# Sequence 0: the last of its four pairs of heads in float16 parts

## The chip, the cores and the metric

The kernel runs on one core of one Trainium2 chip. What counts is the device time of one execution in microseconds. The kernel before was timed in three runs; their median is 1101.2 us (1100.18 to 1104.09).

## The reference

Eight sequences of 576 tokens go through an attention layer with eight heads of 64 channels, and its output through a feed-forward layer (FFN). Each head mixes causal softmax attention with a retrieval from a memory that came in with the sequence:

```python
scores = scale * np.matmul(q, k.transpose(0, 1, 3, 2))
scores = np.where(causal, -1000000000.0, scores)
a = np.exp(scores - scores.max(-1, keepdims=True))
a /= a.sum(-1, keepdims=True) + 1e-09
local = np.matmul(a, v)
q_p = phi(q)                                   # where(q > 0, q, exp(q) - 1) + 1
mem_out = einsum(q_p, M_prev) / (einsum(q_p, z_prev) + 1e-06)
attn = g * mem_out + (1 - g) * local           # g = sigmoid(beta), one per head

h = x @ w_in                                   # 4608 x 512 by 512 x 2048
out = (h * np.clip(h + 3.0, 0.0, 6.0) / 6.0) @ w_out
```

Input and output are float32, except the two FFN weights, which arrive as float64. The kernel works with float16 pairs: a number is a scaled upper half plus a lower half, and a product takes two or three matmuls.

## The kernel before, in words

**Attention.** The 576 tokens of a sequence make five blocks of 128 (the last has 64). Heads go in pairs of two, since two heads of 64 channels fill 128 partitions; pair p is 0 to 3. A *unit* is one head of one pair for one group of query blocks, and the groups are (0, 1), (2,), (3,) and (4,). The units of a sequence follow each other group by group, in each group pair by pair, in each pair head 0 and head 1: 32 units to a sequence. The names carry these numbers, sequence_group_pair_head: sT_0_2_1_0 holds the scores of sequence 0, group (3,), pair 1, head 0.

A unit goes through these steps: `scores` on TensorE (transposed, keys on partitions), `reduce` (a maximum over key blocks on VectorE, for block 0 a copy on ScalarE, then a maximum over partitions on GpSimd, into mb), `sub` on VectorE, `exp` on ScalarE, `pv` on TensorE (values and memory into o), and for the second head `combine`, which divides and adds both heads' parts into x. For sequences from 1 on the exponentials are also split: `exp` makes the upper half ah on GpSimd, `lo` the lower half al on VectorE.

**Two forms of operands.** For sequence 0 all four pairs use float32 operands straight from the load ("nat"). Each pair lies in one of the first four of six slots of SBUF, is loaded in two parts (256 tokens, then 320), and needs only phi(q) in two parts (`nat_phi`, two passes of ScalarE and one of VectorE to a part). For the later sequences `prep_steps` prepares a pair in ten steps: load q, k and v into staging tiles; magnitude passes on ScalarE and a maximum over partitions on GpSimd; scales; then k, q, phi(q) and v are split into two halves (ScalarE the upper, VectorE the lower), and SP copies the halves of k, q and phi(q) into the slot, four copies for each of them. `mem_steps` does the like for the sequence's memory.

**FFN.** Tokens go in 18 blocks of 256. Block 0 (NNAT = 1) is computed in float32: x is transposed by TensorE in two halves (columns of pairs 0 and 1, and of pairs 2 and 3) and copied to x32 by ScalarE; `ffn1` makes eight steps ph_0_0 to ph_0_14 of eight matmuls each, `ffn2` eight steps of four matmuls for two outputs po_0_0 and po_0_1. The float32 weights come out of the float64 words by `w_decode`: 16 chunks, each with a pass of ScalarE (L643), two of VectorE (L644, L645) and a magnitude pass of ScalarE (L646). A raw chunk waits in W2 or in slots 4 and 5; the buffer is loaded again (L630) after that magnitude pass. Later the weights are split too.

**What sets the order.** A scheduler orders each engine's instructions by priorities that the code sets with `at(...)`, by dependencies, and by its own estimate of times. FFN pieces get priorities by block and step, attention units by their due time. On the chip each engine's queue, SP's for the DMAs too, then runs in that order: an instruction that waits holds what is behind it.

## Time and profile before

| | |
|---|---|
| median of three runs | 1101.2 us |
| profiled execution, its own time | 1104.08 us |
| its span on the core | 1102.4 us |
| TensorE (PE) busy | 1071.2 us, 97% |
| VectorE (DVE) busy | 893.0 us, 81% |
| ScalarE (ACT) busy | 789.0 us, 72% |
| GpSimd (POOL) busy | 405.2 us, 37% |
| bytes read from and written to HBM | 48.14 MB, 9.44 MB |

A busy PE is not a PE at its peak: matmuls are pipelined, and their records overlap. What one costs where PE is full is read from start to start of rows, or from a long row with its count. A float32 matmul leaves two records. PEclk is the granted TensorE clock; where the profile has no record of it, it prints full clock, so the spacing of matmuls tells more there. DMA issues stand on SP's queue (SPq), and a long row there is an issue that waits for its buffer.

### The profile page before, as it was taken

The numbers are of one execution on the slowest core, as the hardware profiler recorded it, in microseconds if no ns is written. First come the engines' busy times: TensorE is split into PE (matmuls) and PEld (weight loads), VectorE is DVE, ScalarE is ACT, GpSimd is POOL, SyncE is SP. The second block draws the span as 40 slices with busy tenths as digits, with TensorE's granted clock in tenths as the row PEclk, the third lists the DMA queues.
The fourth block names the chain that finished last, engine by engine and source line by source line (L and its number), as shares of the span: only waits on it lengthen the run. The fifth ranks groups of instructions, "written<-read, shape, count | busy, mean of one in ns | idle before, by whom it ended". The sixth has DMA issues, their size and how long they took to land.

```text
span 1102.4 us, 28691 instructions
## 1 busy us (share of the span) xinstructions
PE 1071.2 (97%) x10728; PEld 788.6 (72%) x10728; DVE 893.0 (81%) x2350; ACT 789.0 (72%) x1884; POOL 405.2 (37%) x544
## 2 busy tenths in 40 slices
PE   7999999899999999999999999999999999999998
PEld 6888758586767776776768686768686858685664
DVE  5989779899899979998989896999699868792321
ACT  4778769778888878788877887778687857563322
POOL 2322123445455434533344533453244433350000
PEclk9999999999999999999999999999999999999999
DMA  8835452334333432443433432332432230101100
GB/s 251 313 110 174 108 148 78 77 85 102 102 97 97 98 106 78 117 92 101 103 102 47 136 99 51 81 102 76 128 82 68 52 77 14 29 10 31 30 10 20
DMA packets 101467, 101.38 MB, mean 92 GB/s; under 512 B 50256, under 2 KB 80976, under 8 KB 101328
## 3 DMA queue, kind: packets, MB, share of 16 engines
q1 hardware_dynamic: 101328, 99.56, 33.6%
q8 instruction: 84, 1.38, 0.6%
q14 instruction: 55, 0.45, 0.1%
HBM read 48.14 MB, written 9.44 MB: 52 GB/s over the span
## 4 chain that ended last, share of the span: by engine, by line
PE 39%; DVE 18%; ACT 5%; issue 5%; DMA 4%; POOL 1%; SPq 1%; DVEq 0%; ACTq 0%; POOLq 0%
PE po L565 6%; PE po L567 6%; PE po L566 6%; PE ph L542 5%; PE ph L543 5%; PE ph L544 5%; DVE rm L371 3%; DVE a L379 3%; DVE al L398 3%; DVE r L551 2%; DVE g L553 2%; PE sT L354 1%; PE sT L355 1%; PE o L425 1%; PE o L423 1%
## 5 line engine op out<-in xcount | busy, mean ns | idle before, releaser
L373 POOL PARTITION_ALL_REDUCE mb<-rm x256 | 253.9, 992 | 354.5 <-DVE rm L371 249.8
L542 PE MATMUL ph<-x,W 128*128 128x256 f16 x1088 | 296.6, 273 | 3.0 <-DMA x<-W 2.2
L543 PE MATMUL ph<-x,W 128*128 128x256 f16 x1088 | 296.6, 273 | 0.0
L544 PE MATMUL ph<-x,W 128*128 128x256 f16 x1088 | 296.6, 273 | 0.0
L565 PE MATMUL po<-W,g 128*128 128x512 f16 x544 | 206.2, 379 | 5.0 <-ACT ot L573 3.5
L567 PE MATMUL po<-W,g 128*128 128x512 f16 x544 | 206.2, 379 | 0.9 <-DVE g L553 0.9
L566 PE MATMUL po<-W,g 128*128 128x512 f16 x544 | 206.2, 379 | 0.0
L390 POOL TENSOR_SCALAR_AFFINE_SELECT ah<-a 128x384 f16<-128x384 f32 (+2 forms) x224 | 138.3, 619 | 183.0 <-ACT a L386 124.3
L386 ACT ACTIVATE a<-a,scal 128x384 f32<-128x384 f32 (+2 forms) x224 | 141.0, 631 | 63.1 <-DVE a L379 54.1
L379 DVE TENSOR_TENSOR a<-sT,mb 128x128 f32<-128x128 f32 (+3 forms) x320 | 148.3, 479 | 25.6 <-POOL mb L373 19.7
L398 DVE TENSOR_TENSOR al<-a,ah 128x384 f16<-128x384 f32 (+2 forms) x224 | 135.5, 605 | 10.7 <-POOL ah L390 9.9
L371 DVE TENSOR_REDUCE rm<-sT 128x128 f32<-128x256 f32 (+3 forms) x256 | 135.0, 527 | 8.3 <-ACT rm L369 3.8
L551 DVE SCALAR_TENSOR_TENSOR r<-r,ph 128x512 f32<-128x512 f32 x136 | 92.0, 677 | 52.5 <-ACT r L550 51.9
L550 ACT ACTIVATE r<-ph,bias_g,gsc 128x512 f32<-128x512 f32 x136 | 106.4, 783 | 33.2 <-PE ph L544 29.4
L355 PE MATMUL sT<-slot 128*128 128x128 f16 (+1 forms) x840 | 126.7, 210 | 0.0
L354 PE MATMUL sT<-slot 128*128 128x128 f16 (+1 forms) x840 | 124.2, 210 | 1.9 <-DVE a L379 1.4
L542 PEld LDWEIGHTS <-W 128*128 128x128 f16 x1088 | 106.4, 98 | 18.1 <-issue 3.0
L423 PE MATMUL o<-slot,ah 128*128 128x65 f16 (+1 forms) x840 | 116.1, 196 | 3.2 <-POOL ah L390 1.6
L543 PEld LDWEIGHTS <-W 128*128 128x128 f16 x1088 | 106.3, 98 | 15.7 <-issue 1.1
L424 PE MATMUL o<-slot,ah 128*128 128x64 f16 (+1 forms) x840 | 115.2, 195 | 0.0
L455 ACT ACTIVATE x<-o,cf 128x64 f32<-128x64 f32 (+1 forms) x280 | 88.0, 314 | 37.4 <-DVE cf L442 37.2
L544 PEld LDWEIGHTS <-W 128*128 128x128 f16 x1088 | 106.3, 98 | 11.7
(157 smaller groups left out, 2297.3 us busy)
## 6 DMA issues: line engine op xcount, KB each, us to landing
slot<-q SPq DMA_DIRECT2D x112, 144.0 KB, 2.5
out<-ot SPq DMA_DIRECT2D x36, 256.0 KB, 2.0
stv<-vn SPq DMA_DIRECT2D x28, 320.0 KB, 3.5
W<-w_in SPq DMA_DIRECT2D x8, 1024.0 KB, 11.2
slot<-w_out SPq DMA_DIRECT2D x8, 1024.0 KB, 5.0
stq<-qT SPq DMA_DIRECT2D x28, 288.0 KB, 3.1
stk<-kT SPq DMA_DIRECT2D x28, 288.0 KB, 3.2
slot<-k SPq DMA_DIRECT2D x112, 72.0 KB, 2.0
```

Source lines behind the costliest of these rows:

```text
L371: DVE.tensor_reduce(rm[:, m0:m0 + nq], src.rearrange("p (t q) -> p q t", q=nq), axis=AX.X, op=ALU.max)
L373: POOL.partition_all_reduce(mb[:, 0:self.m], rm[:, 0:self.m], P, RMAX)
L379: DVE.tensor_tensor(a[:, c0:c0 + w].rearrange("p (t q) -> p t q", q=nq), self.sT[:, c0:c0 + w].rearrange("p (t q) -> p t q", q=nq), self.m ...
L386: self.exp_ins = ACT.activation(a, a, AF.Exp, scale=slots[self.b, self.p]["esc"], bias=LN_SA)
L390: POOL.affine_select(self.ah[:, 0:self.n], a, pattern=[[0, self.n]], compare_op=ALU.is_ge, fill=0.0, base=1, channel_multiplier=0)
L398: DVE.tensor_tensor(self.al[:, 0:n], self.a[:, 0:n], self.ah[:, 0:n], op=ALU.subtract)
L542: PE.matmul(ph[:, m], wh, f["xh"][:, c], start=c == 0, stop=False)
L543: PE.matmul(ph[:, m], wh, f["xl"][:, c], start=False, stop=False)
L544: PE.matmul(ph[:, m], wl, f["xh"][:, c], start=False, stop=c == 3)
L565: PE.matmul(po, gh[:, m, ts], W2[:, m, 0:512], start=m == 0, stop=False)
L566: PE.matmul(po, gh[:, m, ts], W2[:, m, 512:], start=False, stop=False)
L567: PE.matmul(po, gl[:, m, ts], W2[:, m, 0:512], start=False, stop=m == 15)
```

## The change

Pair 3 of sequence 0 takes the path of the later sequences: loaded whole and split by `prep_steps`, ahead of the order in which the others are. Only pairs 0 to 2 (NATP) stay float32. Sequence 0's memory is needed in both forms, so `mem_steps(0)` runs too, into space that the float32 slots 0 and 2 leave free; its results go under mem["split"]. The loads of pair 3 and of the memory come fourth in LOADS, ahead of pair 2's; two tables of step numbers, PREP_0 and MEM_0, place the other steps at units 0 to 4. Mask operands move from slot 3 to slot 1.

```diff
+NATP = 3
...
-LOADS = ((0, 0), (3, 0), (0, 1), (0, 2), (0, 3), (2, 0), (2, 1), (1, 0), (1, 1), (2, 2), (1, 2), (1, 3), (2, 3))
-B_T = (2, 3, 4, 5)
+LOADS = ((0, 0), (3, 0), (0, 1), (4, 3), (0, 2), (2, 0), (2, 1), (1, 0), (1, 1), (2, 2), (1, 2), (2, 3))
+B_T = (2, 3, 4)
+
+PREP_0 = (0, 0, 1, 1, 2, 2, 2, 3, 4, 4)
+MEM_0 = (0, 0, 1, 2)
...
+        if i == 0:
+            m16_raw = free.bitcast(F32)[:, 0:H * (D + 1)]
+        elif i == 2:
+            m16 = free[:, 0:2 * H * (D + 1)].rearrange("p (x h e) -> p x h e", x=2, h=H)
...
+            self.nat = b == 0 and p < NATP
...
-            if self.b == 0:
+            if self.nat:
                 return
             self.ah = p2.tile([P, 512], F16, name=f"ah_{self.id}", tag="ah")
...
-            mt = mem[b]["t"]
+            mt = mem[b if self.nat else b or "split"]["t"]
...
+        elif x == 4:
+            prep0 = prep_steps(0, n)
+            mem0 = mem_steps(0)
+            prep0[0]()
+            mem0[0]()
...
-    for p in range(NP):
+    for p in range(NATP):
         nat_phi(p, 0)
...
+        for fs0, ks in ((mem0, MEM_0), (prep0, PREP_0)):
+            for f, k in zip(fs0[1:], ks[1:]):
+                if k == t:
+                    at(due(t))
+                    f()
```

What the change makes of the engines' queues is not in these lines, so three places are shown, as the two programs issue them. Line numbers of the changed program are 10 or 11 higher.

The first is ACT, around pair 3's first units. Here W1 from W2 (L643, L654) is a weight chunk's first pass, W2,am1 from W1 (L646, L657) its magnitude pass, rm the copy of block 0's scores, a the exponential, x2 the copy of transposed x. Before:

```order
L643 ACTIVATE W1_95<-W2_96 128x1024
L646 ACTIVATE W2_96,am1_189<-W1_95 128x1024
L643 ACTIVATE W1_95<-W2_96 128x1024
L369 ACTIVATE rm_0_0_3_1_426<-sT_0_0_3_1_413 128x128
L646 ACTIVATE W2_96,am1_189<-W1_95 128x1024
L386 ACTIVATE a_0_0_3_0_409<-a_0_0_3_0_409 128x384
L646 ACTIVATE W2_96,am1_189<-W1_95 128x1024
L527 ACTIVATE x2_0_606<-xp_0_0_607 128x512
L386 ACTIVATE a_0_0_3_1_445<-a_0_0_3_1_445 128x384
```

And with the change (qp is phi(q) of pair 3, amm_1 and mz_1 belong to the memory of sequence 1):

```order
L654 ACTIVATE W1_95<-W2_96 128x1024 x2
L657 ACTIVATE W2_96,am1_189<-W1_95 128x1024 x3
L171 ACTIVATE qp_0_3_379<-e_0_3_320,s_0_3_263 128x576
L167 ACTIVATE junk_293,amm_1_291<-stm_1_200 128x512
L167 ACTIVATE junk_295,amm_1_291<-stm_1_200 128x8
L171 ACTIVATE mz_1_332<-stm_1_200,s_m1_327 128x8x64
L171 ACTIVATE mz_1_332<-stm_1_200,s_m1_327 128x8
L380 ACTIVATE rm_0_0_3_0_468<-sT_0_0_3_0_454 128x128
L380 ACTIVATE rm_0_0_3_1_493<-sT_0_0_3_1_479 128x128
L397 ACTIVATE a_0_0_3_0_473<-a_0_0_3_0_473,scal_0_3_268 128x384
L654 ACTIVATE W1_95<-W2_96 128x1024 x2
L538 ACTIVATE x2_0_697<-xp_0_0_698 128x512
```

Pair 3's first scores are now taken up after four whole weight chunks, its own last split and the memory of sequence 1; before they stood between the second and the fourth magnitude pass.

The second is SP, after the first loads (raw weight chunks go to W2_96, slot4 and slot5; stm, stq, stk and stv are sequence 1's). Before:

```order
L630 DMA slot4_106<-w_out 128x2x512
L630 DMA slot5_107<-w_out 128x2x512
L295 DMA stm_1_203<-mz 64x520
L179 DMA stq_1_0_538<-qT 128x576
L179 DMA stk_1_0_540<-kT 128x576
L295 DMA stm_1_203<-mz 64x520
L630 DMA W2_96<-w_in 128x2x512 x4
L181 DMA stv_1_0_542<-vn 128x640
```

With the change, where slot3 receives pair 3's halves:

```order
L225 DMA slot3_105<-k_0_3_273 64x576 x2
L226 DMA slot3_105<-k_0_3_273 64x576 x2
L233 DMA slot3_105<-q_0_3_281 64x2x576 x2
L305 DMA stm_1_200<-mz 64x520
L189 DMA stq_1_0_629<-qT 128x576
L189 DMA stk_1_0_631<-kT 128x576
L305 DMA stm_1_200<-mz 64x520
L641 DMA W2_96<-w_in 128x2x512 x3
L233 DMA slot3_105<-q_0_3_281 64x2x576
L641 DMA W2_96<-w_in 128x2x512
L233 DMA slot3_105<-q_0_3_281 64x2x576
L225 DMA slot3_105<-qp_0_3_379 64x576
```

Head 0's q goes out ahead of the four reloads of W2, head 1's q after the third and the fourth of them, and phi(q) after these.

The third is PE, where the first scores of the unit sT_0_2_2_0 stand (ph is FFN-in, po FFN-out, o values). Before:

```order
L537 MATMUL ph_0_6_766<-x2_0_606,W1_95 128x256 x5
L416 MATMUL o_0_2_0_0_3_910<-slot0_102,a_0_2_0_0_852 128x65 x4
L537 MATMUL ph_0_6_766<-x2_0_606,W1_95 128x256
L563 MATMUL po_0_0_1079<-W2_96,g2_97 128x512 x3
L537 MATMUL ph_0_8_816<-x2_0_606,W1_95 128x256 x2
L350 MATMUL sT_0_2_2_0_1063<-slot2_104 128x128 x3
```

With the change:

```order
L361 MATMUL sT_0_2_1_1_1071<-slot1_103 128x128 x4
L369 LDWEIGHTS slot1_103
L369 MATMUL sT_0_2_1_1_1071<-slot1_103 128x64
L369 LDWEIGHTS slot1_103
L369 MATMUL sT_0_2_1_1_1071<-slot1_103 128x64
L548 MATMUL ph_0_2_758<-x2_0_697,W1_95 128x256 x8
L548 MATMUL ph_0_4_813<-x2_0_697,W1_95 128x256 x7
L361 MATMUL sT_0_2_2_0_1181<-slot2_104 128x128 x3
```

At the same unit the FFN has come to its fifth step (ph_0_8) and three FFN-out matmuls before, and to the third step (ph_0_4) with none of FFN-out after: 34 and 3 matmuls against 23 and 0.

More of the change, by code (lines that the diff above doesn't have):

```diff
@@ L127 @@
             at += n
-        if i < NP:
+        if i < NATP:
             w32 = whole.bitcast(F32)
@@ L132 @@
                             .rearrange("p (t h e) -> p t h e", t=NB, h=2)))
-        else:
+        elif i >= NP:
             raw.append(whole[:, 0:4096])
-        if i == NP - 1:
-            free = whole.bitcast(BF16)[:, 2 * (2 * S + NB * P + NB * 130):]
+        free = whole[:, 2 * (2 * S + NB * P + NB * 130):]
+        if i == 0:
+            m16_raw = free.bitcast(F32)[:, 0:H * (D + 1)]
+        elif i == 2:
+            m16 = free[:, 0:2 * H * (D + 1)].rearrange("p (x h e) -> p x h e", x=2, h=H)
+        elif i == 1:
+            free = free.bitcast(BF16)
             selm = free[:, 0:2 * P].rearrange("p (a k) -> p a k", a=2)
@@ L170, in prep_steps @@
         st = {}
+        mk = b or "split"
         def pad(dst, value):
@@ L201, in scale @@
             DVE.memset(scal[:, 2:3], SA * 1e-9)
-            ACT.activation(scal[:, 3:4], s[:, 3:4], AF.Copy, scale=mem[b]["eps1"])
-            coef = mem[b]["coef"][:, 2 * p:2 * p + 2]
+            ACT.activation(scal[:, 3:4], s[:, 3:4], AF.Copy, scale=mem[mk]["eps1"])
+            coef = mem[mk]["coef"][:, 2 * p:2 * p + 2]
             ACT.activation(coef[:, :, 0], omg[:, 2 * p:2 * p + 2], AF.Copy, scale=i[:, 2:3])
@@ L280, in nat_mem @@
             SP.dma_start(m[D * r:D * r + D, :, r], mz[0].rearrange("d (j h) e -> d j h e", h=2)[:, :, r])
-        coef = small.tile([P, H, 2], F32, name="coef_0", tag="coef", bufs=2)
+        coef = small.tile([P, H, 2], F32, name="coef_n", tag="coef", bufs=3)
         DVE.tensor_copy(coef[:, :, 0], omg)
@@ L291, in load @@
         def load():
-            t = st["t"] = stg.tile([P, NB * P], F32, name=f"stm_{b}", tag="stg")
-            m = st["m"] = t[:, 0:H * (D + 1)].rearrange("p (h e) -> p h e", e=D + 1)
+            t = stg.tile([P, NB * P], F32, name=f"stm_{b}", tag="stg")[:, 0:H * (D + 1)] if b else m16_raw
+            m = st["m"] = t.rearrange("p (h e) -> p h e", e=D + 1)
             for r in range(2):
@@ L306, in conv @@
             s, i = scales(st["amr"], 2, TS, f"m{b}")
-            t = p2.tile([P, 2, H, D + 1], F16, name=f"mz_{b}", tag="mz")
+            t = p2.tile([P, 2, H, D + 1], F16, name=f"mz_{b}", tag="mz") if b else m16
             m = st["m"]
@@ L310, in conv @@
             split(t[:, 0, :, D:], t[:, 1, :, D:], m[:, :, D:], s[:, 1:2])
-            coef = small.tile([P, H, 2], F32, name=f"coef_{b}", tag="coef", bufs=2)
+            coef = small.tile([P, H, 2], F32, name=f"coef_{b}", tag="coef", bufs=3)
             DVE.tensor_scalar(coef[:, :, 1], gate, s[:, 1:2], i[:, 0:1], op0=ALU.mult, op1=ALU.mult)
@@ L314, in conv @@
             DVE.tensor_scalar_mul(eps1, s[:, 1:2], 1e-6)
-            mem[b] = dict(t=t, s=s, coef=coef, eps1=eps1)
+            mem[b or "split"] = dict(t=t, s=s, coef=coef, eps1=eps1)
         return [load, lambda: None, absmax, conv]
@@ L338, in scores @@
             h = self.h
-            if self.b == 0:
+            if self.nat:
                 t = nat[self.p]
+                r = slice(D * h, D * h + D)
             else:
@@ L347, in scores @@
                     o = sT[:, c0 + j * nq:c0 + (j + 1) * nq]
-                    if self.b == 0:
-                        r = slice(D * h, D * h + D)
+                    if self.nat:
                         PE.matmul(o, t["k"][r, j * P:(j + 1) * P], t["q"][r, q0:q0 + nq],
@@ L355, in scores @@
                         PE.matmul(o, kk, qhl[sl][:, 1, h, q0:q0 + nq], start=False, stop=j < i)
-                    if j == i and self.b == 0:
+                    if j == i and self.nat:
                         for a in range(nq // D):
@@ L386, in exp @@
             self.exp_ins = ACT.activation(a, a, AF.Exp, scale=slots[self.b, self.p]["esc"], bias=LN_SA)
-            if self.b == 0:
+            if self.nat:
                 return
@@ L393, in lo @@
         def lo(self):
-            if self.b == 0:
+            if self.nat:
                 return
@@ L413, in pv @@
                 cs = [slice(c0 + j * nq, c0 + (j + 1) * nq) for j in range(i + 1)]
-                if b == 0:
+                if self.nat:
                     for j in range(i + 1):
@@ L711 @@
     am2 = const.tile([P, 8], F32, name="am2")
-    for p in range(NP):
+    for p in range(NATP):
         nat_phi(p, 0)
@@ L770 @@
                         plan.setdefault(t + k, []).append(f)
-        for p in range(NP):
+        for fs0, ks in ((mem0, MEM_0), (prep0, PREP_0)):
[3 more added lines that the diff above has]
+                    f()
+        for p in range(NATP):
             if t == B_T[p]:
```

## The prediction

> **What bounds the kernel now.** I read the slices of the page first, then a table of windows, then the timelines of PE, ACT and SP over the first 90 us, where all that the change touches lies. The slices, and the windows that I cut at the turns of the start (us, busy us of PE, PEld, DVE, ACT and POOL, PEclk, DMA share, GB/s):
>
> ```profile
> PE   7999999899999999999999999999999999999998
> DVE  5989779899899979998989896999699868792321
> ```
> ```profile
> 0.00:41.00 41.00, 32.33 (x155) 28.99 (x156) 28.02 (x111) 21.74 (x46) 11.98 (x19) 1.00 0.91 287
> 41.00:62.00 21.00, 21.00 (x89) 18.75 (x89) 16.75 (x43) 18.16 (x38) 6.14 (x8) 1.00 0.46 179
> 62.00:89.00 27.00, 27.00 (x154) 21.84 (x153) 24.61 (x56) 19.64 (x33) 6.38 (x7) 1.00 0.48 158
> 89.00:141.00 52.00, 51.42 (x335) 39.73 (x334) 44.99 (x119) 38.99 (x75) 10.70 (x14) 1.00 0.46 133
> 141.00:163.00 22.00, 20.10 (x99) 10.33 (x97) 14.85 (x40) 15.52 (x33) 6.62 (x6) 0.92 0.57 147
> 163.00:300.00 137.00, 132.66 (x1513) 99.86 (x1512) 125.59 (x337) 113.14 (x292) 63.02 (x82) 1.00 0.35 93
> ```
>
> From 62 us on PE is filled to 51.42 of 52 and 132.66 of 137 us, with DVE close behind (125.59 of 137). So whatever PE has not done at some point of the program is paid at the end, nearly one for one. Ahead of 62 us it is otherwise. PE handled 89 records in 21 us, then 154 in 27, and its busy time there is not work at full speed:
>
> ```profile
> 18.20 1.20 PE L350 MATMUL sT<-slot 64*128 64x128 f32 x4
> 60.80 5.50 PE L537 MATMUL ph<-x,W 128*128 128x256 f32 x20
> 66.22 1.04 PE L350 MATMUL sT<-slot 64*128 64x128 f32 x8
> 69.78 5.45 PE L537 MATMUL ph<-x,W 128*128 128x256 f32 x24
> 85.16 2.74 PE L563 MATMUL po<-W,g 128*128 128x512 f32 x6
> 88.69 0.93 PE L350 MATMUL sT<-slot 64*128 64x128 f32 x6
> ```
>
> A float32 matmul is two records. Four score records took 1.20 us at 18.20 (0.30 each), eight took 1.04 at 66.22 (0.13 each): PE runs at about half speed until the FFN's dense stretch at 60.80. That stretch starts when block 0 has all its x columns, and these include pair 3's. One FFN-in matmul costs 5.45 / 12 = 0.454 us, one FFN-out matmul 2.74 / 3 = 0.913 us. The start is therefore a race of ACT, DVE, POOL and SP to give PE the FFN, and pair 3 is the last runner in it.
>
> **The change part by part.** *What ACT does earlier.* ACT's timeline ahead of the FFN, and its and DVE's groups (count, busy us, mean ns, idle before):
>
> ```profile
> 21.10 0.47 ACT L268 ACTIVATE slot<-slot 128x320 f32<-128x320 f32 x1 [5.33 <-DMA slot<-qT]
> 36.91 0.51 ACT L386 ACTIVATE a<-a 128x384 f32<-128x384 f32 x1
> 38.65 1.06 ACT L646 ACTIVATE W<-W 128x1024 f32<-128x1024 f32 x1 [1.24 <-DVE cf L441]
> 41.08 0.95 ACT L386 ACTIVATE a<-a 128x384 f32<-128x384 f32 x2
> 56.59 0.57 ACT L527 ACTIVATE x<-xp 128x512 f32<-128x512 f32 x1
> 73.64 0.51 ACT L386 ACTIVATE a<-a 128x384 f32<-128x384 f32 x1
> ```
> ```profile
> L643 ACT ACTIVATE W<-W 128x1024 f32<-128x1024 f32 x8 | 9.0, 1121 | 0.0
> L646 ACT ACTIVATE W<-W 128x1024 f32<-128x1024 f32 x8 | 8.4, 1047 | 3.9 <-DVE cf L441 2.0 <-DVE W L645 1.8
> L158 ACT ACTIVATE junk<-stq 128x576 uint8<-128x576 f32 x3 | 2.0, 678 | 1.5 <-DMA stq<-qT 1.5
> L162 ACT ACTIVATE k<-stk,s 128x576 f16<-128x576 f32 x2 | 1.5, 760 | 0.0
> L234 ACT ACTIVATE e<-stq 128x576 f32<-128x576 f32 x2 | 1.4, 675 | 2.7 <-DMA slot<-qp 2.7
> L268 ACT ACTIVATE slot<-slot 128x256 f32<-128x256 f32 x4 | 1.7, 416 | 4.1 <-DMA slot<-qT 4.1
> L163 DVE SCALAR_TENSOR_TENSOR k<-stk,s,k 128x576 f16<-128x576 f32 x2 | 1.6, 808 | 0.0
> ```
> ```profile
> L373 POOL PARTITION_ALL_REDUCE mb<-rm x60 | 62.5, 1041 | 131.8 <-DVE rm L371 89.4 <-DVE cf L441 19.2 <-DVE cf L440 9.7
> L390 POOL TENSOR_SCALAR_AFFINE_SELECT ah<-a 128x384 f16<-128x384 f32 x16 | 10.2, 641 | 16.2 <-ACT a L386 11.7 <-DVE s_m L151 2.5 <-issue 1.4
> ```
>
> Ahead of the fourth weight chunk's magnitude pass (the row at 38.65, over at 39.8 with its accumulator read) ACT gains four long magnitude passes (q, k, v and the memory, about 0.68 each, 2.7), five splits (k, q, v at 0.76 to 0.82, the memory in two, 3.2), pair 3's two phi passes over 576 columns (1.4) and some 0.8 us of small ones, and loses its four passes on slot 3 (2 x 0.416 and 2 x 0.46 = 1.75): +6.4 us. Its cover is the 5.33 us in which ACT waits for slot 0's second part. Not all of that can be used, since pair 3's and the memory's own loads, two maxima on POOL and the scales on DVE lie between the passes. I take 3 us left over (bounds 1 and 6.4): the fourth pass ends at about 42.8. DVE's share (four lower parts of pair 3 at 0.81, two of the memory, the scales: some 6 us) fits its own idle there (28.02 busy of 41).
>
> *What stands ahead of pair 3.* By the new order ACT then does pair 3's last split (0.76) and the memory of sequence 1 (two magnitude passes, a POOL maximum, the scales, two splits: about 3 us) before it touches pair 3's first scores, so these start at 46.5. SP's timeline shows why they could hardly be sooner:
>
> ```profile
> 30.49 9.71 SPq L630 DMA_DIRECT2D W<-w_in  x4
> ```
>
> The four loads of raw weight chunks hold SP until chunks 0 to 3 are through ACT's magnitude pass. Head 1's two copies of q now stand behind three and four of them, and qp's four behind those: at 41 to 43 us, plus landing. Behind head 1's scores PE's queue holds the first (2,) units of pair 0, so PE stands still meanwhile. From 46.5 the chain is a reduction (0.4), POOL's maximum (1.04), the subtraction (0.7) and the exponential: 49.5 for head 0, where the row of before stands at 36.91. Head 1 waits for POOL again and for two weight chunks on DVE: about 55, against 41.08.
>
> *From there to the FFN.* Between the fourth pass and the second copy of x (the row at 56.59) ACT's new order has 8 L643 (9.0), 6 L646 with their reads (6.3), 7 exponentials (3.6), 5 magnitude passes (3.4) and about 4 us of others: 26 us, and I add 5 for the waits above and for pair 3's normalisation on DVE, which stands behind five more weight chunks there. 42.8 + 31 gives 74 (70 to 78). The twelve instructions from there to the last exponential of the (2,) units come to 7 us: 81 where before has 73.64. This unit belongs to pair 3, so POOL's copy (0.64) and DVE's difference (0.6) follow before PE may go on: the FFN's second step starts at 84. It and seven eighths of the third (15 x 0.454 = 6.8) bring PE to the first scores of the unit sT_0_2_2_0 at **91**, bounds 87 and 95. Before is there at 88.69: **+2.3 us** (-1.7 to +6.3).
>
> *What PE has not done by then.* At this place before has issued 34 FFN-in and 3 FFN-out matmuls, the change 23 and none (the order's third pair of rows): 11 x 0.454 + 3 x 0.913 = **+7.7 us** of PE work that is still to come. This count is read, not guessed.
>
> *What PE is spared.* Pair 3's units of (3,) and (4,) come after this place:
>
> ```profile
> 97.58 1.16 PE L350 MATMUL sT<-slot 64*128 64x128 f32 x8
> 99.69 1.00 PE L416 MATMUL o<-slot,a 128*128 128x65 f32 x8
> 100.53 0.44 PE L418 MATMUL o<-m_nat,slot 128*128 128x130 f32 x2
> 118.63 1.32 PE L350 MATMUL sT<-slot 64*128 64x64 f32 x10
> 123.51 1.38 PE L416 MATMUL o<-slot,a 128*64 128x65 f32 x20
> 124.73 0.39 PE L418 MATMUL o<-m_nat,slot 128*64 128x130 f32 x2
> ...
> 161.63 0.22 PE L354 MATMUL sT<-slot 128*128 128x128 f16 x1
> 161.69 0.22 PE L355 MATMUL sT<-slot 128*128 128x128 f16 x1
> ...
> 163.54 0.19 PE L423 MATMUL o<-slot,ah 128*128 128x65 f16 x1
> 163.57 0.20 PE L424 MATMUL o<-slot,ah 128*128 128x64 f16 x1
> ```
>
> In float32 the two heads of a (3,) unit cost 2 x (1.16 + 1.00) + 0.44 = 4.8, of a (4,) unit 2 x 1.32 + 1.38 + 0.39 = 4.4. In float16 the starts are 0.06 apart for scores and 0.03 for values: 2 x (9 x 0.06 + 14 x 0.03) = 1.9 and 2 x (11 x 0.03 + 17 x 0.03) = 1.7, with the 64-column scores taken like the values. Spared: 5.6 us. It counts only where PE is what the queue waits for. In 89 to 141 us DVE is busy 44.99 of 52 and gets four more differences, so I take half, **-3 us** (bounds 0 and -5.6). The units of (0, 1) and (2,) save more, but PE waits there for ACT and DVE, so I count nothing; they are in the 91. Transfers: pair 3 whole and the memory once more add about 0.3 MB to what is loaded, hidden by the weight loads. On POOL two more maxima, of the memory and of pair 3, stand between the maxima of the first units; their wait is in the 3 us left over above.
>
> Sum: 2.3 + 7.7 - 3 = **+7 us**. On the profiled execution, 1104.08, that is 1111; this execution was the slow end of the runs shown, so on their median of 1101.2 I forecast **1108**. With every bound at its good end 7.7 - 1.7 - 5.6 = +0.4, at its bad end 7.7 + 6.3 = +14: the likeliest case's own range is 1103 to 1115.
>
> [...]
>
> **The rivals.** *Faster: the lag fills holes.* The FFN work that is left over is ready whenever PE waits. Before lost 1.9 us in 141 to 163 us and a clock of 0.92 on top (0.08 x 22 = 1.8), and 4.3 us in 163 to 300. If the 7.7 us goes into these 8 us of holes and the start shifts by -1.7 with 5.6 spared, the sum is 0.4 - 7.7 = -7: 1094. It decides if PE is filled to over 99% from 141 to 300 us. For it: the units are cheaper and the weights' decoding is one chunk further at that place. Against: PE's queue is in order and those holes are waits on ACT and DVE, which get no less work. *No change.* ACT's waits are shorter than I made them and half the spared time is real: 7.7 - 1.7 - 4 = +2, 1103. *Much slower: DVE binds the middle.* If DVE, at 44.99 of 52 already, sets the pace to 160 us, nothing is spared and the late start is felt in full: 2.3 + 7.7 + 3 or 4 for PE's waits = +13, 1114. *The change does not do what it says*: not so, the new order holds pair 3's loads fourth and its float16 units in all four groups.
>
> **How the numbers follow.** Forecast 0.48, no change 0.23, much slower 0.14, faster 0.15. A measurement of this kernel can tell about 0.5% from no change, 5.5 us: 1095.7 to 1106.7. Slower: 0.14 and three quarters of the forecast, 0.50. Faster: 0.14, nearly all of that rival. Within: the rest, 0.36. The range leaves out the better half of the faster case and the far end of the slowest: 1095 to 1116.
>
> **What would show it.** Right: in the new profile the second copy of x (L538) near 74 us, the first exponential with scal_0_3 (L397) near 50, sT_0_2_2_0's scores near 91, PE full from there. Wrong in the first term if that copy comes before 65; wrong in the second if PE's idle time between 141 and 300 us shrinks by more than 4 us; wrong in the third if DVE's busy share in 90 to 140 us passes 95%.

## The result, and the profile after

The changed kernel takes **1133.92 us** (median; 1133.09 to 1136.08), the kernel before, on the same chip, 1102.08 (1100.18 to 1104.09): a ratio of 1.0292, with an interval of 1.0266 to 1.0317. The change costs 32 us. The forecast was 1108 with a range of 1095 to 1116; the side was right, the size was not. The profiled execution took 1133.09 us with a span of 1131.4.

The slices of the page, PE and DVE, in forty equal parts of the span:

```profile
PE   6289999999999999999999999999999999999998
DVE  6489988999799967997889887999889968792321
```

Before, the first five digits of PE were 79999. Now PE is busy for less than three tenths of the second slice, 28 to 57 us. The table of windows, cut where the prediction cut it (us, busy us of PE, PEld, DVE, ACT and POOL, PEclk, DMA share, GB/s):

```profile
0.00:41.00 41.00, 22.80 (x109) 20.12 (x109) 29.55 (x118) 27.00 (x59) 9.34 (x18) 1.00 0.93 297
41.00:62.00 21.00, 6.49 (x39) 5.58 (x39) 5.18 (x15) 5.09 (x11) 3.08 (x5) 1.00 0.68 228
62.00:89.00 27.00, 22.22 (x129) 18.83 (x127) 25.82 (x60) 23.32 (x43) 12.91 (x12) 0.97 0.21 80
89.00:141.00 52.00, 51.28 (x349) 41.49 (x347) 48.27 (x119) 42.55 (x80) 13.76 (x19) 0.95 0.52 162
141.00:163.00 22.00, 22.00 (x155) 15.97 (x155) 19.57 (x60) 16.30 (x34) 9.09 (x10) 1.00 0.43 111
163.00:300.00 137.00, 131.43 (x1411) 93.46 (x1411) 124.19 (x332) 110.45 (x273) 63.16 (x79) 0.99 0.37 97
```

From 41 to 62 us every compute engine stands still most of the time: 6.49 us of PE, 5.18 of DVE, 5.09 of ACT in 21. The DMA engines do not, at 0.68. From 89 us on PE is filled as before.

The timeline of PE has the reason, at pair 3's first scores (start, length, line, names, count, and in brackets the idle time before and what ended it):

```profile
37.65 0.27 PE L365 MATMUL sT<-slot 128*128 128x128 f16 x1 [1.60 <-DMA slot<-q]
54.73 0.29 PE L366 MATMUL sT<-slot 128*128 128x128 f16 x1 [16.82 <-DMA slot<-q]
```

The first matmul of head 0's scores (with q's upper half) runs at 37.65, the second (with q's lower half) waits 16.82 us for a copy of q. The other engines wait behind it; ACT's timeline:

```profile
38.53 1.06 ACT L657 ACTIVATE W<-W 128x1024 f32<-128x1024 f32 x1 [0.79 <-DVE cf L452]
55.76 0.28 ACT L380 ACTIVATE rm<-sT 128x128 f32<-128x128 f32 x1 [11.38 <-PE sT L372]
58.59 0.61 ACT L397 ACTIVATE a<-a,scal 128x384 f32<-128x384 f32 x1
64.09 0.61 ACT L397 ACTIVATE a<-a,scal 128x384 f32<-128x384 f32 x1
86.02 0.57 ACT L538 ACTIVATE x<-xp 128x512 f32<-128x512 f32 x1
```

And SP's timeline shows which copy it is, with the landing times of copies issued in the first 110 us below it (name, count, KB each, median us from issue to landing):

```profile
26.98 3.07 SPq L233 DMA_DIRECT2D slot<-q  x2
...
37.55 1.56 SPq L641 DMA_DIRECT2D W<-w_in  x3
39.16 0.93 SPq L233 DMA_DIRECT2D slot<-q  x1
40.19 0.71 SPq L641 DMA_DIRECT2D W<-w_in  x1
40.95 0.65 SPq L233 DMA_DIRECT2D slot<-q  x1
```
```profile
W<-w_in SPq DMA_DIRECT2D x8, 1024.0 KB, 8.5
slot<-q SPq DMA_DIRECT2D x4, 144.0 KB, 10.9
slot<-k SPq DMA_DIRECT2D x4, 72.0 KB, 11.2
```

Head 0's copies went out at 26.98, head 1's at 39.16 and 40.95, behind three and four weight loads of 1024 KB. Head 1's two copies took 11.7 and 13.7 us from issue to landing, and each landed within 1 us of the weight load ahead of it (at 50.9 and 54.7 us, the loads at 50.0 and 54.2). PE went on at 54.73, 13.8 us after the last copy was issued. That head 0's matmul waits for head 1's copies is a matter of address ranges: a copy for one head writes both parts of q (`qhl[..., :, h]`), so head 1's range begins inside head 0's. The scheduler counts that as an overlap, and the second part of head 0 waits for the later writer.

### The profile page after: what moved, and what is told of

Same layout as the page of the kernel before. It is cut to its first block, busy times and chain, and to the rows that moved or that the text cites. A ratio compares the mean times of both kernels' runs of the same rounds, so it can differ in the third digit from the quotient of the medians.

```text
span 1131.4 us, 28849 instructions
## 1 busy us (share of the span) xinstructions
PE 1067.7 (94%) x10760; PEld 780.7 (69%) x10760; DVE 903.4 (80%) x2373; ACT 795.4 (70%) x1901; POOL 413.1 (37%) x554
## 4 chain that ended last, share of the span: by engine, by line
PE 35%; DVE 9%; ACT 3%; issue 3%; DMA 2%; POOL 1%; SPq 0%; DVEq 0%; ACTq 0%; POOLq 0%
PE po L576 5%; PE po L577 5%; PE po L578 5%; PE ph L553 4%; PE ph L554 4%; PE ph L555 4%; DVE al L409 1%; DVE a L390 1%; PE sT L365 1%; PE sT L366 1%; PE o L434 1%; DVE rm L382 1%; PE o L436 1%; DVE r L562 1%; DVE g L564 1%
## 5 line engine op out<-in xcount | busy, mean ns | idle before, releaser
L401 POOL TENSOR_SCALAR_AFFINE_SELECT ah<-a 128x384 f16<-128x384 f32 (+2 forms) x232 | 145.4, 629 | 209.0 <-ACT a L397 116.6
L397 ACT ACTIVATE a<-a,scal 128x384 f32<-128x384 f32 (+2 forms) x232 | 145.8, 629 | 49.4 <-DVE a L390 41.4
L409 DVE TENSOR_TENSOR al<-a,ah 128x384 f16<-128x384 f32 (+2 forms) x232 | 141.2, 609 | 12.0 <-POOL ah L401 11.3
L366 PE MATMUL sT<-slot 128*128 128x128 f16 (+1 forms) x870 | 134.1, 211 | 16.8 <-DMA slot<-q 16.8
L365 PE MATMUL sT<-slot 128*128 128x128 f16 (+1 forms) x870 | 133.4, 212 | 4.3 <-DVE a L390 2.3
L562 DVE SCALAR_TENSOR_TENSOR r<-r,ph 128x512 f32<-128x512 f32 x136 | 91.8, 676 | 55.0 <-ACT r L561 54.7
L434 PE MATMUL o<-slot,ah 128*128 128x65 f16 (+1 forms) x870 | 122.3, 196 | 12.1 <-ACT y L467 7.1
L561 ACT ACTIVATE r<-ph,bias_g,gsc 128x512 f32<-128x512 f32 x136 | 106.1, 781 | 31.8 <-PE ph L555 25.5
L435 PE MATMUL o<-slot,ah 128*128 128x64 f16 (+1 forms) x870 | 121.0, 195 | 0.0
L563 ACT ACTIVATE g<-r 128x512 f16<-128x512 f32 x136 | 86.2, 635 | 47.3 <-DVE r L562 47.2
```

Of the source, the lines that this page charges most:

```text
L366: PE.matmul(o, kk, qhl[sl][:, 1, h, q0:q0 + nq], start=False, stop=j < i)
L397: self.exp_ins = ACT.activation(a, a, AF.Exp, scale=slots[self.b, self.p]["esc"], bias=LN_SA)
L409: DVE.tensor_tensor(self.al[:, 0:n], self.a[:, 0:n], self.ah[:, 0:n], op=ALU.subtract)
```

## A ledger of PE's time

Two numbers from the matmul records serve for all runs below. *Own work* is the sum over records of the distance from one start to the next, counted at most up to the usual distance for that form (its 20th percentile in the trace of before). *Holes* are what the distances exceed this by; half rate counts as a hole. Both together are the time from PE's first matmul to its last. Holes are cut at the first scores of sequence 1 and of sequence 4. Before: own work 1004.8, holes 37.6, 26.0 and 25.3; the table gives differences from these. Since a distance below the usual one counts as it is, own work varies by 1 us between orders of the same matmuls. "Full rate" is where the spacing of float32 records falls to half (63 us in the kernel before); "FFN late" is how much FFN work (0.454 and 0.913 us a matmul in float32; in float16 0.11 and 0.22 from start to start, about a quarter) stands later in the written order at the first scores of sequence 3 than it does before. Times are medians against the kernel before in the same group of runs.

| kernel | time, us | against before | own work | holes seq. 0 | 1 to 3 | 4 to 7 | full rate | FFN late |
|---|---|---|---|---|---|---|---|---|
| changed | 1133.9 | +31.8 | -8.1 | +28.6 | +6.8 | +1.6 | 80 us | 14 us |
| W reloads behind q (e1) | 1122.1 | +17.4 | -9.0 | +18.7 | +3.3 | +4.1 | 69 | -6 |
| all weight loads behind q (e2) | 1104.8 | +0.1 | -7.6 | +10.2 | +2.5 | -3.9 | 72 | 3 |
| q copies by part (e4) | 1123.0 | +18.2 | -8.1 | +17.4 | +8.8 | +0.3 | 83 | 15 |
| e2 and e4 together (f2) | 1119.0 | +15.6 | -8.8 | +18.8 | +6.6 | -2.3 | 83 | 9 |
| no preparation (e3) | 1116.2 | +11.4 | -7.6 | +11.8 | +5.3 | +2.8 | 77 | 13 |
| no preparation, mask first (g1) | 1107.8 | +4.3 | -8.2 | +5.6 | +3.5 | +3.0 | 57 | -2 |
| before, two loads later (f1) | 1121.0 | +17.6 | -0.7 | +1.9 | +14.0 | +1.7 | 68 | 15 |
| before, the same further on (g3) | 1116.6 | +13.1 | +1.1 | +4.2 | +3.8 | +2.0 | 72 | 14 |
| before, two loads exchanged (g2) | 1108.5 | +5.0 | +0.1 | +0.9 | +2.7 | -0.9 | 71 | 7 |
| before, pair 3 late (g4) | 1109.0 | +5.5 | -0.2 | +2.1 | +3.9 | +0.1 | 68 | 10 |

The changed kernel's row adds up: -8.1 + 28.6 + 6.8 + 1.6 = 28.9, and the spans differ by 1131.4 - 1102.4 = 29.0. At usual distances pair 3's float32 matmuls cost 15.0 us, and the float16 matmuls in their place cost 6.6. So the float16 units do spare PE some 8 us; the holes of sequence 0 take more than three times that back, and 8.4 us more are lost later.

## The experiments

**Weight loads behind the copies (e1, e2).** The reloads of W2 (chunks 4 to 7), and in e2 also the first two chunks of the second weight (8 and 9), are requested only behind pair 3's last q copy:

```diff
-        SP.dma_start(w_raw(n)..., src...)
+        with tc.issue_after(last_q[-1].ins) if 4 <= n < 8 else nullcontext():   # e2: n < 10
+            SP.dma_start(w_raw(n)..., src...)
```

Expected of e1:

> Edit: on SP the four reloads of raw weight chunks 4 to 7 stand behind the last of pair 3's q copies; the w_out chunks 8 and 9 stay ahead of all copies. Theory A (late landing): the 16.8 us in which PE waits for q copies, with ACT 11.4 us and DVE 10.9 us idle behind it, come from head 1's copies being queued and landing behind four 1 MB weight loads. Then the wait shrinks to about 4 us (head 0's copies land at 37.6, head 1's some 3 us later), pair 3's first scores end near 42 instead of 55, and the time falls by 12 to 14 us, to about 1120. Theory B (amount of work): pair 3's preparation on ACT and DVE is what is late, the wait only shows it; then the time stays at 1130 or over.

Expected of e2:

> Edit: as e1, and the two w_out chunks 8 and 9 also stand behind the last q copy. Theory A: even head 0's copies (issued at 27 to 30 us, landed at 37.6) no longer share the DMA engines with 2 MB of w_out, all q copies land by about 33, PE does not wait for them, 15 to 18 us come back: 1116 to 1119. Theory B: 1130 or over.

Measured: e1 1122.13 us, a ratio of 1.0170 (1.0139 to 1.0200); e2 1104.84, 1.0005 (0.9987 to 1.0024). PE's waits at pair 3's first scores, e1 and then e2:

```profile
37.82 0.26 PE L368 MATMUL sT<-slot 128*128 128x128 f16 x1 [2.06 <-DMA slot<-q]
42.43 0.29 PE L369 MATMUL sT<-slot 128*128 128x128 f16 x1 [4.34 <-DMA slot<-q]
```
```profile
33.46 0.27 PE L368 MATMUL sT<-slot 128*128 128x128 f16 x1 [1.55 <-DMA slot<-q]
38.38 0.29 PE L369 MATMUL sT<-slot 128*128 128x128 f16 x1 [1.61 <-DMA slot<-q]
```

The wait of 16.82 us becomes 4.34, and 1.61 when the two 1024 KB loads ahead of the k copies are gone too. In e2 part of that wait is filled: PE does value matmuls of other units between the two rows, and head 0's second matmul runs 4 us sooner than in e1. e1 came as theory A had it, e2 ended 11 us below theory A's range, which the shorter wait alone doesn't explain. With the loads out of the way the change costs nothing, in this order of the rest; f2 below shows how much hangs on that order.

**The overlap alone (e4).** The loads stay where they are; each q copy of pair 3 is split by part:

```diff
-                    SP.dma_start(qhl[sl][D * r:D * r + D, :, h], t[D * h:D * h + D])
+                    for x in range(2) if b == 0 else (slice(None),):
+                        SP.dma_start(qhl[sl][D * r:D * r + D, x, h], t[D * h:D * h + D, x])
```

> Edit: each of pair 3's four q copies is made as two, one for the upper and one for the lower halves, so that a copy of head 1 no longer spans addresses of head 0; nothing is reordered by hand. Theory A': the q copies of head 1 are late because, as written, they overlap head 0's in range, wait for those to land (37.6 us) and so stand behind the weight reloads; then all eight copies go out one after the other ahead of the reloads, PE's wait shrinks to about 4 us and the time is near e1's, 1118 to 1122. If the overlap does not matter: 1132 to 1135.

Measured: 1122.95 us, 1.0175 (1.0144 to 1.0206), as expected. PE at the first two units of pair 3:

```profile
37.59 0.26 PE L366 MATMUL sT<-slot 128*128 128x128 f16 x1 [1.70 <-DMA slot<-k]
40.24 0.26 PE L366 MATMUL sT<-slot 128*128 128x128 f16 x1 [1.59 <-DMA slot<-q]
```

Pair 3 starts no sooner than in the changed kernel, but the next group starts at 40.4 us instead of 55.7. Without the overlap the scheduler also puts head 1's copies ahead of the weight loads, since they need not wait for head 0's to land, so the overlap and this order are tested together.

**Both repairs (f2).** The edits of e2 and e4 together.

> The changed kernel, with both repairs: the reloads of the first weight and the first two chunks of the second are requested behind pair 3's last q copy, and each q copy of pair 3 is split by its two parts, so that head 0's copies share no address range with head 1's. With the first repair alone PE still waited 1.55 and 1.61 us for q copies at pair 3's first scores, and was 10 us behind the kernel before there. Theory A (what is left at pair 3 is the two waits): 2 to 4 us below that repair alone, 1101 to 1103 us. Theory B (what is left is the chain load, maximum, split, copy itself, and the order of the rest): within 2 us of 1105 us.

Measured: 1118.97 us, 1.0144 (1.0120 to 1.0168), against both theories: 14 us slower than e2, although pair 3 starts 1 us sooner. PE's timeline shows a third of this at the first FFN step:

```profile
69.09 2.04 PE L552 MATMUL ph<-x,W 128*128 128x256 f32 x4 [4.80 <-DVE z L461]
```

In this order the FFN's first matmuls wait 4.80 us for a normalisation on DVE, with all of PE's queue behind them; in e2 they ran without a wait:

```profile
60.78 2.07 PE L551 MATMUL ph<-x,W 128*128 128x256 f32 x4
```

Neither repair touches that normalisation or the FFN; the order of both moved with the rest. By the ledger the difference from e2 is 8.6 us of holes in sequence 0 and 5.7 behind it; what makes the others was not found.

**No preparation (e3, f3, f4, g1).** These leave out the magnitudes, splits and copies of pair 3 and of the float16 memory; constants stand in the slot:

```diff
-        for fs0, ks in ((mem0, MEM_0), (prep0, PREP_0)): ...
+            for d in (kst[3], qhl[3], qps[3], vst[3], m16):
+                POOL.memset(d, 0.03125)
```

> Leaves out pair 3's and the memory's preparation (magnitudes, scales, splits, copies): slot 3 and the split memory hold a constant from the start, so pair 3's values of sequence 0 are not the reference's. The loads, the order tables and the float16 units with their POOL copies and DVE differences stay. It shows the gain side alone. If what PE is spared by float16 units counts where PE is full (5.6 us for the two late groups, more with the early ones), 1094 to 1098, against 1102 before. If DVE and POOL, which get eight differences and copies more, take it back, 1100 to 1104.

Measured: 1116.16 us, 1.0119 (1.0088 to 1.0150): slower than before although nothing of the preparation is left, which neither theory had. One part of it is the experiment's own fault. POOL's timeline, and the wait it makes on PE:

```profile
1.81 6.20 POOL L723 MEMSET slot<- 128x1280 f16 x5
```
```profile
11.30 0.26 PE L369 MATMUL sT<-slot 64*128 64x64 bf16 x2 [3.25 <-DVE slot L702]
```

POOL writes the constants from 1.8 to 8.0 us, ahead of the mask that the first scores need. Two more runs were to mend that. f3 places the constants at a later unit; f4 adds f1's later loads (below):

> The changed kernel without the preparation of pair 3 and of the float16 memory of sequence 0 (no magnitudes, no splits, no copies; constants stand in their places, so the output is not the reference's), as in the run before that left it out, but with the constants written after the first eight units' masks are made: there POOL wrote them from 1.8 to 8.0 us, ahead of the mask that the first scores wait for, and PE's second group started 6.2 us late. The float32 loads of pair 3 stay. Theory A (that late mask was carried to the end): 1109 to 1112 us. Theory B (the float16 units have PE do about 15 us less, and without preparation this is gained): 1090 to 1098 us. Theory C (PE's saved work turns into waiting, since other engines set the pace of the first 140 us, and a few us more are lost by the order of later work): 1100 to 1108 us.

> As the run without preparation and with late constants, and beside it the first two chunks of the second weight are requested behind the first reload of the first weight (the edit that is tried on the kernel before in the same group of runs). If that place is worth something only to pair 3's copies, this is within 2 us of the run without the edit; if it is worth 5 us or more by itself, it is that much below.

Measured: f3 1115.72 us, 1.0115 (1.0091 to 1.0139), f4 1116.42, 1.0115 (1.0065 to 1.0166). POOL still wrote the constants at 1.81 us in both, so the premise of these two expectations was wrong and they decide nothing about the mask. They say that f1's edit, which costs the kernel before 17 us, costs nothing here. (The 15 us in f3's expectation are what pair 3's float32 matmuls cost; 8 are spared.) g1 then forces the constants behind the mask:

```diff
+            with tc.issue_after(mask.ins):
+                for d in (kst[3], qhl[3], qps[3], vst[3], m16):
+                    POOL.memset(d, 0.03125)
```

> The changed kernel without the preparation of pair 3 and of the float16 memory of sequence 0 (constants in their places, so the output is not the reference's), now with the constants forced behind the making of the mask: in the two runs that left the preparation out they were still written ahead of it, and PE's third pair was 6 us late. Theory A (the 4 us by which that put pair 3 late were carried to the end): 1110 to 1113 us. Theory B (the saved work of PE is gained once nothing is late): 1088 to 1097 us. Theory C (any move of the order costs about 10 us in sequences 1 to 3, and the saved work is lost to waiting in the first 140 us): 1108 to 1118 us, and pair 3's first scores within 1 us of the kernel before.

Measured: 1107.83 us, 1.0038 (1.0025 to 1.0051), just below theory C's range; against its own before it is 7 us better than e3, and how much of that is the mask and how much the order that moved with it isn't told apart. Pair 3's first scores were 2.2 us late, not within 1. What matters is the ledger's row: with no preparation at all, own work falls by 8.2, and holes of sequence 0 grow by 5.6. **Two thirds of PE's saving come back as holes of sequence 0**, and the 6.5 us of holes behind it are more than what is left. Which engine makes these holes was not told apart.

**Neighbours of the kernel before (f1, g2, g3, g4).** f2 and e3 made the order itself a suspect. In f1 the two first chunks of the second weight are requested behind the first reload of W2, in g3 behind all four; in g2 two entries of LOADS change places; in g4 pair 3's loads wait for the fifth unit's exponential. All compute what the kernel before computes:

```diff
+        with tc.issue_after(w4[0].ins) if n in (8, 9) else nullcontext():     # f1; g3: behind reload 7
             SP.dma_start(w_raw(n)..., src...)
-LOADS = (..., (1, 2), (1, 3), (2, 3))                                          # g2
+LOADS = (..., (1, 2), (2, 3), (1, 3))
+            with tc.issue_after(units[4].exp_ins.ins):                         # g4
+                nat_load(3, 0)
+                nat_load(3, 1)
```

> The kernel before, with one edit: the first two chunks of the second weight (1 MB each raw load pair) are requested behind the first reload of the first weight instead of ahead of it, at the place where they stand in the run whose weight loads all wait for pair 3's copies. Nothing of sequence 0's pair 3 changes. Theory A (the later loads gained there only because they cleared the way for the copies of pair 3, which this kernel doesn't have): 1102 to 1106 us, as before. Theory B (the place of these two loads is worth 5 us or more by itself): 1090 to 1098 us.

> The kernel before, with two neighbours of the table of loads exchanged: the fourth chunk of the first weight is requested ahead of pair 3's second part instead of behind it. Nothing is added or left out. If the order of the kernel before is a favourable one, and neighbours of it cost what the two moved loads of the second weight cost (17 us), 1110 to 1122 us; if that run was a special case, 1101 to 1106 us.

> The kernel before, with the first two chunks of the second weight requested behind all four reloads of the first weight (behind the first reload in the run that cost 17 us). Same question as the run with the two exchanged loads: 1110 to 1122 us if most neighbours of the order of before are that much slower, 1101 to 1106 us if not.

> The kernel before, all float32, with pair 3's loads requested only behind the exponential of the fifth unit, so that its first scores come some 5 to 10 us late, as they do in the changed kernel with the copies ahead of the weights. Nothing else is changed. If a late start of pair 3 is carried to the end, 1107 to 1112 us; with a moved order's cost on top, 1115 to 1125 us; if the later work takes it up, 1101 to 1105 us.

Measured: f1 1121.01 us, 1.0152 (1.0125 to 1.0180); g2 1108.47, 1.0043 (1.0028 to 1.0059); g3 1116.58, 1.0117 (1.0098 to 1.0136); g4 1109.04, 1.0046 (1.0023 to 1.0070). f1 is the plainest: up to the first scores of sequence 1 it is 2 us behind, and it loses 14 in sequences 1 to 3, where nothing was edited. The table of PE's waits from 143 to 500 us, before and then f1 (who waits <- for whom: us, times, longest):

```profile
PE o L425 <- DVE al L398: 1.2, 4, 0.4
PE o L423 <- ACT y L456: 0.5, 3, 0.2
```
```profile
PE o L424 <- ACT y L457: 8.0, 5, 4.8
PE o L426 <- DVE al L399: 4.6, 5, 1.9
```

In f1 the value matmuls wait for ACT to empty their accumulators (8.0 us, once 4.8) and for DVE's lower halves. In the changed kernel the same two rows read 4.8 and 2.9. So four different small moves cost the kernel before 5 to 17.6 us, and none made it faster. Of g4's 5.5 us little is the late start itself: pair 3 is 5.4 us late, but the first unit of the next group is 0.8 us early, and the units after it are 0.8 to 1.1 us late.

**Is it the late FFN? (h1 to h4).** In most of the slower kernels FFN work stands later in the order, and attention ahead. One edit moves the FFN's first three blocks forward, in f1 (h1), in the changed kernel (h2), in f2 (h3) and, as control, in the kernel before (h4):

```diff
-        at(16 * n + k)
+        at(16 * n + k - (12 if n < 3 else 0))
         if not ffn_step():
```

> The kernel before with the two moved loads of the second weight (17 us slower than before), and beside it the first three blocks of the FFN get priorities 12 steps earlier. In the written order this takes away the postponement of FFN matmuls: at the first scores of sequence 3, 15 us of them stood behind their place in the kernel before, now -2 us. Theory L (the loss is that late FFN work: attention runs ahead until its buffers stop it, then FFN alone is left): 1103 to 1109 us. Theory N (the loss is spread over small waits that any other order has, whatever the FFN's place): 1115 to 1123 us.

> The changed kernel with only the first three FFN blocks' priorities 12 steps earlier: FFN matmuls behind their place in the kernel before at the first scores of sequence 3 fall from 14 us to -2 us; at the first scores of sequence 1 they stay (9 us). The 17 us wait at pair 3's scores stays. Theory L (late FFN work costs some 8 of the 32 us): 1121 to 1127 us. Theory N: 1130 to 1136 us.

> The changed kernel with both repairs of pair 3's copies (weight loads behind them, q copies split by part; 1119 us) and the first three FFN blocks' priorities 12 steps earlier (FFN work behind its place at the first scores of sequence 3: 9 us without, 0 with). Theory L: 1108 to 1113 us. Theory N: 1116 to 1122 us.

> The kernel before with only the first three FFN blocks' priorities 12 steps earlier, the control of that edit. FFN work stands 1 to 7 us ahead of its place in sequences 1 to 3. Theory L: within 3 us of before or faster, 1098 to 1106 us. Theory N (any other order than this one is slower): 1108 to 1120 us.

Measured: h1 1114.64 us (1.0104, 1.0070 to 1.0138), h2 1128.21 (1.0223, 1.0197 to 1.0248), h3 1123.22 (1.0177, 1.0150 to 1.0203), h4 1111.06 (1.0071, 1.0044 to 1.0097). By the medians h1 and h2 gain 6 us on their originals; h1 ends at the edge of theory N's range, h2 between the two. h3 loses 4 on f2, just above theory N's range, and the control loses 7, as theory N has it. Late FFN work seems to be a part of the loss in two kernels and is not the rule. In six of six neighbours of the kernel before (f1, g2, g3, g4, h1, h4) the time rises, by 5 to 17.6 us; one mechanism for all of them was not found. The record doesn't say whether the kernel before had been picked as the fastest of many orders; if it had, slower neighbours are what to expect.

**PE's rate (i1, i2).** In the kernel before and in the changed one PE's float32 rows take half rate until well into sequence 0. Before, and then changed:

```profile
58.92 1.54 PE L416 MATMUL o<-slot,a 128*128 128x65 f32 x6
67.89 1.55 PE L416 MATMUL o<-slot,a 128*128 128x65 f32 x12
```
```profile
75.28 1.65 PE L361 MATMUL sT<-slot 64*128 64x128 f32 x6 [0.76 <-DVE a L390]
80.01 1.61 PE L427 MATMUL o<-slot,a 128*128 128x65 f32 x12
```

Before has 0.26 us a record at 58.92 and 0.13 at 67.89; the change still 0.27 at 75.28. Two kernels put nine matmuls of 512 columns on zeros into the kernel before, which nothing reads: i1 at the very start, i2 at about 40 us.

```diff
+    for _ in range(9):
+        PE.matmul(o, gh[:, 0, 0:P], gh[:, 0:2, :], start=True, stop=True)
```

> The kernel before with nine matmuls of 512 columns on zeros, which nothing reads, at PE's start, while it waits for the first loads (until 4.6 us). In the rows of all runs PE works at half rate from the start to the FFN's first dense stretch (62 us in the kernel before, 79 with the change). Theory W (a dense start brings full rate and it stays, since there is work from then on): the float32 score rows take 0.13 us a record instead of 0.26 from 5 us on, and the end comes 5 to 10 us earlier, 1093 to 1099 us. Theory V (rate falls back at the first waits of 2 to 5 us): the rows from 9 us on take 0.26 as before, and the time is 1102 to 1106 us, or more if the order is moved.

> The kernel before with the same nine matmuls at about 40 us, behind the ninth unit's exponential, where PE has no more long waits but still works at half rate. They cost some 3.9 us themselves at half rate. Theory W: full rate from about 45 us instead of 62, which spares up to 8 us of PE's time, so 1097 to 1101 us; if the first 60 us are set by the other engines and not by PE's rate, 1104 to 1108 us, and with a moved order's cost 1108 to 1120 us. Either way the rows tell whether it is dense work that brings full rate: the float32 score records behind the nine take 0.13 us if so, 0.26 if not.

Measured: i1 1117.50 us, 1.0132 (1.0098 to 1.0166); i2 1109.18, 1.0041 (1.0017 to 1.0066). PE's rows around the nine, i2 and then i1:

```profile
31.58 1.62 PE L350 MATMUL sT<-slot 64*128 64x128 f32 x6
...
40.97 4.00 PE L788 MATMUL sT_warm<-g 128*128 128x512 f16 x9
...
47.62 0.82 PE L350 MATMUL sT<-slot 64*128 64x128 f32 x6
...
55.58 1.61 PE L350 MATMUL sT<-slot 64*128 64x128 f32 x6
...
57.23 7.47 PE L537 MATMUL ph<-x,W 128*128 128x256 f32 x22
```
```profile
1.25 4.02 PE L675 MATMUL sT_warm<-g 128*128 128x512 f16 x9 [1.25 <-DVE g L672]
...
6.90 0.69 PE L350 MATMUL sT<-slot 64*128 64x128 f32 x4
...
11.85 1.20 PE L350 MATMUL sT<-slot 64*128 64x128 f32 x4
```

In i2 the rows behind the nine matmuls are at full rate (1.62 us for six records becomes 0.82), but it does not stay: at 55.58, behind a wait of 0.98 us, it is 1.61 again, and in i1, behind a wait of 3.52 us, the rows are back at half rate by 11.85 (1.20 us for four records, 0.69 at 6.90), as theory V has it; the 14 us that i1 loses fit theory V only with a moved order. In i2 the unit sT_0_1_2_0 starts at 48.6 against 48.3 before, so full rate has paid for the nine (4.00 us) by then, and the FFN's dense stretch starts at 57.23 where before has it at 60.80. This fits the prediction's table, where PE has no wait from 41 to 62 us (21.00 busy of 21.00): there its rate does set the pace. The gain is not kept: the first scores of sequence 1 come 4.0 us late, and the whole takes 6 us longer, as theory W has it for a moved order. The order of the two kernels differs, so what a full rate without that would be worth was not measured.

## Why the prediction was wrong

**The first term, the shift at the place of sT_0_2_2_0 (+2.3 us, bounds -1.7 and +6.3), failed**, and most of it failed at one step: "at 41 to 43 us, plus landing", and from it "these start at 46.5". The order was read rightly: head 1's copies do stand behind three and four weight loads, and SP issued them at 39.16 and 40.95, sooner than I said. But the landing was never priced. The one sentence on transfers is about pair 3's own loads and calls them "hidden by the weight loads"; the copies stand behind those loads and are not hidden but late. They needed 11.7 and 13.7 us. The first 110 us of the trace of before have both prices for transfers of this size on this queue, for a copy of q and for the memory of sequence 1, which stands among the weight loads (KB each, median us from issue to landing):

```profile
slot<-q SPq DMA_DIRECT2D x2, 144.0 KB, 3.4
stm<-mz SPq DMA_DIRECT2D x2, 130.0 KB, 12.0
```

Nor did I see that head 0's scores, whose own copies landed at 37.5, would wait for them too. The chain up to the exponentials then ran as priced, only 9 us late: they came at 58.59 and 64.09 (49.5 and 55 were forecast). The stretch behind them was sized too short by 5.5 us: the second copy of x came at 86.02 (74), the scores of sT_0_2_2_0 at 105.61 (91):

```profile
105.61 0.93 PE L361 MATMUL sT<-slot 64*128 64x128 f32 x6
```

Against 88.69 this is +16.9, where +2.3 was said: 9.1 us more by the late landing, 5.5 by the stretch behind it. In that stretch DVE was busy 25.82 of 27 us (62 to 89), and PE's waits in it end mostly on DVE (3.5 of 4.8 us), so the 5 us that I had added for waits were too few; no run tests this part alone. By e4's ledger row splitting the copies, with the order that comes with it, is worth 11 of the 29 us of holes in sequence 0, and 13.6 us of the time.

The trace of the changed kernel, as far as one run can show it, has no transfer that overtook another there: the 144 KB copies took a median of 10.9 us, and all that SP issued from 20 to 51 us landed in the order of issue. The loads issued at 37.55, 38.18, 38.69 and 40.19 landed at 44.1, 46.6, 50.0 and 54.2 us, the copies issued at 39.16 and 40.95, in that order among them, at 50.9 and 54.7.

**The steps on ACT ahead of it held, or better.** The fourth magnitude pass was to end at 42.8; the row at 38.53 ends at 39.6. Since all of ACT's added work was done in time, the bounds of 1 and 6.4 us around it were spent on the wrong place.

**The second term, +7.7 us of FFN work not done, held as a count**: at this place the changed kernel has done 46 records of FFN-in and none of FFN-out, 23 and 0 matmuls. I had also said what would prove it wrong, PE's idle time from 141 to 300 us shrinking by over 4; it went from 6.2 us (1.90 + 4.34) to 5.6 (0 + 5.57). The faster rival, in which the lag fills those holes, is out by the same rows.

**The third term, -3 us for float16 units, was right in size, and its reason is not shown.** From this place to the end own work grows by 4.4 us in the ledger's terms; with 7.7 of late FFN work in it, PE is spared 3.3. I had halved 5.6 because of DVE; its share in 90 to 140 us is 46.50 of 50, 93%, and the 95% that I had set as a mark were not reached.

**What was missing altogether** is a price for moving the order of an engine-filling schedule. From this place to the end holes grew by 7.5 us, for which the sum has no term; with it the account closes: 16.9 + 7.7 - 3.3 + 7.5 = 28.8, and the spans differ by 29.0. All of it lies behind sequence 0, where holes grew by 6.8 + 1.6 us. Neighbours of the kernel before that change no work lost there between 1.8 and 15.7 us (g2 and f1 in the table). That the moved order costs these 8.4 us is a likely reading and not a shown one, since the changed kernel's order after 145 us cannot be had without its start. My largest rival, "much slower", ended at 1114 and put DVE in that place.

**On PE's half rate**, which the prediction read from the rows ahead of 60.80, the runs show two things that don't go together. In i2 rows at full rate followed on nine float16 matmuls that took 4.00 us. In the kernel before PE was busy 21.00 of 21.00 us from 41 to 62, nearly all of it with float32 matmuls, and six records at 58.92 still took 1.54 us. What sets these apart is open. What full rate from the start would be worth is not tested either, since i2 gains up to 57 us and then loses more in another order.

What stays open: why neighbours of this order differ by up to 17 us, why e2 and f2, both free of the long wait, differ by 14, and how much of the changed kernel's later loss is its own. No version was faster than the kernel before; e2 equals it.

## What to carry to other kernels

When an order shows a small copy behind large loads on one queue, price its landing by what is ahead of it (here 11.7 and 13.7 us behind three and four loads of 1024 KB), and ask for each consumer which other writers share its address range: a strided destination can tie two heads together that share no byte, as with the 16.82 us that head 0's second matmul waited here. In a schedule that fills an engine to 97%, as this one does PE, price any edit of the order itself, by timing one or two neighbours that change no work; a gain smaller than their scatter says little about the edit. Work spared on the fullest engine need not come off the time: here 5.6 of 8.2 us came back as holes in the stage where it was spared, even without the preparation.

## What the runs showed of the hardware

PEclk alone did not tell PE's rate. In the kernel before it reads 1.00 from 41 to 62 us, where six value records took 1.54 us (58.92), and 1.00 from 62 to 89, where twelve took 1.55 (67.89). e3 and f3 issue the same matmuls in the same order; their windows from 28 to 55 us:

```profile
28.00:55.00 27.00, 22.37 (x121) 19.78 (x120) 25.09 (x64) 20.51 (x37) 9.37 (x10) 1.00 0.81 281
```
```profile
28.00:55.00 27.00, 21.69 (x122) 19.23 (x120) 25.08 (x64) 20.48 (x38) 9.27 (x10) 0.62 0.80 284
```

PEclk is 1.00 in the one and 0.62 in the other, and PE did nearly the same work: 121 records in 22.37 us busy and 122 in 21.69. From 55 to 83 us it is 1.00 and 0.63, and the rows up to 71 us take the same time, such as twelve value records 2.66 us at 63.94 in e3 and at 64.04 in f3.

Full rate was not always kept through PE's waits. After the changed kernel first came to full rate, its windows of half a microsecond show a PEclk of 0.50 in five stretches, each of six whole windows and parts of one or two more, about 3.4 us, as from 193.0 to 196.4 us around waits of 0.82, 0.80 and 0.62. The kernel before has one such stretch, from 144.8 to 148.2 us behind a wait of 1.59. That makes some 17 us against 3.4; at half rate I estimate the difference at (17 - 3.4) / 2, some 7 us of PE's time.
